# A gated mix of windowed attention and a Mish MLP on one core: tiles read back from DRAM land in the matmul operand itself, and the second half is ordered anew

## The chip, the core and the metric

The kernel runs on one core of a Trainium2 chip. TensorE (PE) multiplies matrices out of SBUF into seven PSUM banks of 128 x 512 fp32; VectorE (DVE), ScalarE (ACT) and GpSimd (POOL) do the elementwise work; SyncE (SP) issues most of the transfers between SBUF and DRAM. Each engine goes through its own list of instructions in order and waits where an instruction needs something that isn't there yet. The metric is the device time of one execution in microseconds.

## The reference

What must be computed, all in fp32, for 2048 tokens of 640 features (x is used by both branches; B_x is not read):

```python
qkv = (x @ wqkv).reshape(B, S, 3, H, Dh)            # 32 heads of 20
idx = pos[:, None] - (jnp.arange(8) * 2)[None, :]   # 8 keys, every second token back
logits = einsum("bhsd,bhswd->bhsw", q, k[idx]) * Dh ** -0.5   # -1e9 where idx < 0
a = einsum("bhsw,bhswd->bhsd", softmax(logits), v[idx]) @ wo
h = x @ w1 + b1                                     # 640 -> 1728
b = (h * tanh(softplus(h))) @ w2                    # Mish, 1728 -> 640
g = sigmoid((x * gate_w).sum(-1, keepdims=True))
out = g * a + (1 - g) * b
```

## The kernel before

**Numbers.** A fp32 product is made of three matmuls in a faster rounding format. Each operand is therefore a *pair*: a tile [128, 2, 512] whose first half (hi) is the rounded value and whose second half (lo) is the rest. `split` makes a pair out of a plain tile: ACT copies it into hi (L400), and DVE or POOL subtracts hi from the plain tile into lo (L403). `mm3` then issues hi by hi (L441), hi by lo (L442) and lo by hi (L443).

**Front half.** The projections of q, k and v, the first MLP layer and the attention run together. The attention is nearly all DVE's (products of 128 x 2560 at L494 and L532, their sums at L497, L542 and L543), 32 pieces of it. The MLP's first layer runs in blocks of 2 x 2 (`quad`) after a Strassen-like scheme with fewer products; ACT copies partial sums from bank to bank between the products (L887) and applies Mish (L695), and for some blocks negates it (L698). Each activation is an activation of another table than the exponential of the softmax (L519), and ACT loads a table (ACT_TABLE_LOAD) where the two meet. The Mish results and sums of them are stored as blocks in DRAM (`act*`, `actt*`). The last 64 of the 1728 columns of a token block are made apart (`mlp1_rest`, "M" and a number in the lists below) in tiles of 64 x 512, whose order of tokens is changed by way of DRAM (`h*`). Sums of w2's quarters (`sums_of_w2`, "S" and a number) go to DRAM too (`s*`).

**Second half.** `mlp2` runs seven products (named a, b, c, e, g, d, f, in this order), each over seven blocks of 128 rows of w2: w2 or its sums (`s*`) as weights, the stored blocks (`act*`, `actt*`) as the moving operand. `load_step` brings in each step's tiles, three steps ahead. A transfer lands in a staging buffer, and `split` makes the pair from it. The last block of three of the products has only 64 rows; there both halves of the tile hold the same 64 rows, one as hi and one as lo, so that two matmuls do for three (`load_low_w`, `load_low_act`, L1207 and L1208). After a product its banks are copied to SBUF (`after_product`, L1106) and, as a start value, back into the bank of a later product. The output projection with wo ("P" and a number, "W") and the gate's rows ("G") come in between, with the stored attention output (`o*`) as moving operand.

**Buffers.** Buffers come from rings: 23 pairs, and as staging 9 `raw`, 3 `hb` and 3 `z`, which also hold Mish results. A buffer is taken again when all that read it is done.

**What sets the order.** `Plan` is a list scheduler with estimated durations. Each engine's tasks are taken by rank, then by when TensorE is estimated to need them; a task of kind "ANY" (mostly lo) goes to DVE or to POOL, whichever the rules `NEAR`, `TURN`, `HOP` give it to. TensorE's tasks come in the order written in the string `FRONT` and, for the second half, in `mlp2`; `BACK` says at which step of `mlp2` the small works are asked for ("1M2": M2 at step 1). Both `EARLY_S` and `HELD` shift when a kind of task may go. All of this is decided when the program is built. On the chip each list is fixed, and semaphores make the waits.

## Time and profile before

| | us |
|---|---|
| median of 3 runs | 624.73 (624.44 to 624.84) |
| the profiled execution | 628.4 |
| its span | 626.3 |
| PE busy, matmul | 617.0 (99%) |
| DVE busy | 565.2 (90%) |
| ACT busy | 384.2 (61%) |
| POOL busy | 255.3 (41%) |

A row of the trace's timeline has the start in us from the span's start, the duration, the engine, the line of the kernel, the operation, output <- inputs, the shape, a count, and in brackets how long the engine was idle before it and what ended that. A row of waits has the waiting operation, the one waited for, the sum in us, how often, and the longest. The durations of matmuls are modelled and overlap; the distance of their starts tells how fast they go. "SPq" is SP's issue of a transfer, and the last number in a row of transfers is the time to its landing. The profiled execution is longer than the median of the others.

### The profile page before, as it was taken

Reading aid. Unit: us, or ns where it says so; the run is one execution under the profiler, and the core shown is the slowest. Engines: PE = TensorE matmul, PEld = TensorE weight load, DVE = VectorE, ACT = ScalarE, POOL = GpSimd, SP = SyncE. Lnnn points to the kernel's source line nnn. Section 1 sums busy time; section 2 is a strip of 40 time slices with the busy share of each in tenths; the row PEclk is TensorE's granted clock in tenths of the full one; section 3 lists DMA queues with packets and bytes.
Section 4 is the critical chain, followed back from the end, with each engine's and each line's share of the span. In section 5 each row is a group of like instructions: output and inputs, shape, how many; then the busy total and the mean of one; then the engine's idle time right before and its main releaser. Section 6 shows DMA issues by size and latency. Waiting matters only on the chain.

```text
span 626.3 us, 8954 instructions
## 1 busy us (share of the span) xinstructions
PE 617.0 (99%) x2717; PEld 509.8 (81%) x2717; DVE 565.2 (90%) x581; ACT 384.2 (61%) x851; POOL 255.3 (41%) x250
## 2 busy tenths in 40 slices
...
GB/s 307 254 200 197 93 235 279 262 255 225 333 265 290 148 289 308 231 203 256 282 295 214 313 211 229 201 239 281 341 332 297 199 259 233 260 252 172 138 1 169
DMA packets 100609, 149.47 MB, mean 239 GB/s; under 512 B 11456, under 2 KB 47296, under 8 KB 100528
## 3 DMA queue, kind: packets, MB, share of 16 engines
...
q8 instruction: 21, 0.34, 0.2%
...
## 4 chain that ended last, share of the span: by engine, by line
PE 87%; DVE 5%; DMA 4%; issue 2%; POOL 1%; ACT 1%; SPq 1%; DVEq 0%; POOLq 0%; ACTq 0%
PE bank L443 28%; PE bank L441 28%; PE bank L442 28%; DMA act<-z 1%; PE bank L587 1%; POOL pair L403 1%; DVE pr L494 1%; DVE pair L403 1%; DMA raw<-act 1%; PE bank L383 1%; PE bank L1208 1%; DMA hb<-act 1%; PE bank L1207 1%; DMA z<-act 0%; DVE pr L542 0%
## 5 line engine op out<-in xcount | busy, mean ns | idle before, releaser
L442 PE MATMUL bank<-pair 128*128 128x512 f32 (+2 forms) x812 | 314.8, 388 | 2.1 <-DVE pair L403 2.0
L441 PE MATMUL bank<-pair 128*128 128x512 f32 (+2 forms) x812 | 314.4, 387 | 0.0
L443 PE MATMUL bank<-pair 128*128 128x512 f32 (+2 forms) x812 | 314.3, 387 | 0.0
L403 POOL TENSOR_TENSOR pair<-raw,pair 128x512 fp32r<-128x512 f32 (+3 forms) x104 | 130.9, 1270 | 190.9 <-DVE side L536 47.3
L442 PEld LDWEIGHTS bank<-pair 128*128 128x128 f32 x812 | 152.5, 188 | 32.8 <-DVE pair L403 3.0
L441 PEld LDWEIGHTS bank<-pair 128*128 128x128 f32 x812 | 152.5, 188 | 30.6 <-ACT bank L887 0.5
L443 PEld LDWEIGHTS bank<-pair 128*128 128x128 f32 x812 | 152.6, 188 | 30.0 <-POOL pair L403 0.2
L400 ACT ACTIVATE pair<-raw 128x512 fp32r<-128x512 f32 (+3 forms) x198 | 117.0, 611 | 44.4 <-DMA raw<-act 19.7
L532 DVE TENSOR_TENSOR pr<-kvq,side 128x2560 f32<-128x2560 f32 x32 | 90.2, 2820 | 1.0
L497 DVE TENSOR_REDUCE lg<-pr 128x128 f32<-128x2560 f32 x32 | 90.1, 2817 | 0.7
L494 DVE TENSOR_TENSOR pr<-kvq,side 128x2560 f32<-128x2560 f32 x32 | 90.1, 2815 | 0.5
L403 DVE TENSOR_TENSOR pair<-raw,pair 128x512 fp32r<-128x512 f32 (+3 forms) x94 | 62.7, 690 | 7.3 <-ACT pair L400 7.0
L593 ACT ACTIVATE kvq<-bank 128x320 f32<-128x320 f32 x64 | 27.9, 437 | 46.8 <-PE bank L443 46.8
L542 DVE TENSOR_TENSOR pr<-pr 128x1280 f32<-128x1280 f32 x32 | 48.7, 1522 | 0.8
L400 ACT ACTIVATE pair<-hb 128x512 fp32r<-128x512 f32 (+2 forms) x40 | 24.7, 617 | 19.8 <-DMA hb<-actt 11.7
L403 POOL TENSOR_TENSOR pair<-hb,pair 128x512 fp32r<-128x512 f32 x12 | 15.6, 1301 | 42.3 <-PE bank L443 12.5
L887 ACT ACTIVATE bank<-bank 128x512 f32<-128x512 f32 x36 | 21.0, 584 | 16.0 <-PE bank L443 15.9
L441 PE MATMUL bank<-kvq,pair 128*128 128x512 f32 x72 | 28.3, 393 | 1.6 <-ACT bank L887 1.6
L443 PE MATMUL bank<-kvq,pair 128*128 128x512 f32 x72 | 28.3, 393 | 0.1
L442 PE MATMUL bank<-kvq,pair 128*128 128x512 f32 x72 | 28.1, 390 | 0.0
L740 POOL TENSOR_TENSOR raw<-raw 128x256 f32<-128x256 f32 (+1 forms) x24 | 20.4, 875 | 17.8 <-DVE side L536 8.2
L683 POOL DMA_DIRECT2D actt<-actt x26 | 22.4, 862 | 12.7 <-DVE pair L403 7.8
...
## 6 DMA issues: line engine op xcount, KB each, us to landing
raw<-in_w SPq DMA_DIRECT2D x34, 256.0 KB, 4.8
raw<-actt SPq DMA_DIRECT2D x30, 256.0 KB, 4.0
...
raw<-in_x SPq DMA_DIRECT2D x29, 256.0 KB, 5.4
actt<-hb SPq DMA_DIRECT2D x28, 256.0 KB, 4.0
act<-z SPq DMA_DIRECT2D x24, 256.0 KB, 6.4
actt<-z SPq DMA_DIRECT2D x24, 256.0 KB, 6.0
raw<-act SPq DMA_DIRECT2D x23, 256.0 KB, 4.7
```

Of the source, the lines that this page charges most:

```text
L400: a = add("ACT", act_ns(n), lambda: A.activation(hi(), raw(), AF.Copy), after, rank=rank, take=take, hold=hold, kind="hi")
L403: return (V if e == "DVE" else G).tensor_tensor(lo(), raw(), hi().bitcast(F32), op=OP.subtract)
L441: nc.tensor.matmul(ps, ah, bh, start=first, stop=False, skip_group_check=more)
L442: nc.tensor.matmul(ps, ah, bl, start=False, stop=False, skip_group_check=more)
L443: nc.tensor.matmul(ps, al, bh, start=False, stop=last, skip_group_check=more)
L494: return V.tensor_tensor(pr, window(kv, s0, 0), qs[:, :, None, :].to_broadcast([128, 2, W, QF]), op=OP.mult)
L497: return V.tensor_reduce(lg_w[:, s0:s0 + 2], pr.rearrange("p s w (h d) -> p s w h d", d=DH), op=OP.add, axis=AX.X)
L532: return V.tensor_tensor(pr.rearrange("p s w (h d) -> p s w h d", d=DH), vw, pw[:, :, :, :, None].to_broadcast([128, 2, W, HQ, DH]), op=OP ...
L542: step("DVE", 1495, lambda: V.tensor_tensor(pr[:, :, 0:4], pr[:, :, 0:4], pr[:, :, 4:8], op=OP.add))
L593: a = add("ACT", 330, lambda: A.activation(kv[:, 7 + s], ps.t[:, QF:3 * QF].rearrange("p (a b) -> p a b", a=2), AF.Copy), [done] + before, ...
L683: return add("POOL", 1200, lambda: G.dma_start(out=blk[key][:rows], in_=src(), accum_op=OP.add, max_dma_last_dim=2048), after, rank=-0.5, ...
L887: return add("ACT", 590, lambda: A.activation(to.t, of.t, AF.Copy), after, rank=-0.6, take=[to], hold=[of], kind=kind)
```

## The change

A class `Landing` gives a loaded tile its place. With `inner` off it is as before: a staging buffer, and a pair that is taken when the split begins. With `inner` on the transfer takes the pair itself and lands in the second half of it; hi is copied out of there, and lo is made over the landed values in place. It is on for what the program itself stored: the Mish blocks, the sums of w2 and the attention output. The program's inputs still land in staging. In `load_low_w` the memset of the unused quarter waits for DVE's subtraction where the tile landed there.

Beside this there are 2 `hb` and 4 `z`, the strings `FRONT` and `BACK` and the numbers `EARLY_S`, `TURN`, `HOP` and `HELD` are new, and the constant 3 of the steps loaded ahead has a name (`DEEP`). Lines after the class have numbers that are 19 higher (L403 is L404, L441 to L443 are L460 to L462, L695 is L714, L887 is L906, L1106 is L1118).

```diff
-SIZES = {"pair": 23, "home": 6, "raw": 9, "hb": 3, "z": 3}
-FRONT = """q1 Q00 s0 w0 Q01 r00 r10 q2 Q10 F0 F1 Q11 r20 r40 T00 T10 Q20 T20 r30 Q21 q3 T30 T40 S0 Q30 w1
-r50 q4 T50 y3 x2 s1 Q31 F2 r01 Q40 F3 M0 T01 r11 r21 q5 r31 r51 M1 T11 S3 Q41 r41 T21 Q50 T31
-Q51 q6 S2 T41 q7 Q60 S1 S4 T51 H Q61 Q70 Q71"""
-BACK = "1M2 1M3 43P4 0S6 2S5 31P1 26W 22G 35P0"
-EARLY_S = 4000
+SIZES = {"pair": 23, "home": 6, "raw": 9, "hb": 2, "z": 4}
+FRONT = """q1 Q00 s0 w0 Q01 r00 q2 r10 r20 Q10 F0 F1 Q11 T00 T10 Q20 r40 S0 T20 r30 Q21 q3 T30 T40 Q30 w1
+r50 y3 q4 T50 x2 s1 Q31 F2 r01 Q40 F3 M0 T01 r11 r21 q5 r31 r51 M1 T11 S3 Q41 r41 T21 Q50 T31
+Q51 q6 T41 S2 q7 Q60 S1 T51 H Q61 Q70 Q71 S4"""
+BACK = "20G 26P1 1S5 6M3 35P0 46P4 18W 1S6 0M2"
+EARLY_S = 2000
+DEEP = 3
...
-    NEAR, TURN, PATIENCE, HOP, STAY, HELD = 4500, 2200, 11000, 3712, 3000, 24502
+    NEAR, TURN, PATIENCE, HOP, STAY, HELD = 4500, 1760, 11000, 3711, 3000, 11176
...
-    def load_pair(src, eng, n=512, rank=SOON, drank=0.0, after=(), wide=False, home=None, cols=1):
-        raw, p = stage(wide), home or pair_buf()
-        d = dma(lambda: raw.t[:, :n].rearrange("p (a f) -> p a f", a=cols) if cols > 1 else raw.t[:, :n], src, after, rank=drank, take=[raw], size=n * 512)
-        p.ready = split(lambda: raw.t[:, :n], lambda: p.t[:, 0, :n], lambda: p.t[:, 1, :n], n, [d], eng, [raw], [p], rank)
-        return p
+    class Landing:
+        def __init__(self, inner, n, home=None, wide=True):
+            self.p, self.n, self.inner = home or pair_buf(), n, inner
+            self.raw = None if inner else stage(wide)
+            self.take = [self.p if inner else self.raw]
+            self.later = [] if inner else [self.p]
+            self.hold = [self.p] if inner else [self.raw, self.p]
+
+        def at(self, rows=slice(0, 128), a=0, b=None):
+            b = self.n if b is None else b
+            return self.p.t[rows, 1, a:b].bitcast(F32) if self.inner else self.raw.t[rows, a:b]
+
+        def split(self, after, eng, rank=SOON):
+            p, n = self.p, self.n
+            return split(self.at, lambda: p.t[:, 0, :n], lambda: p.t[:, 1, :n], n, after, eng, self.hold, self.later, rank)
+
+    def load_pair(src, eng, n=512, rank=SOON, drank=0.0, after=(), wide=False, home=None, cols=1, inner=False):
+        to = Landing(inner, n, home, wide)
+        d = dma(lambda: to.at().rearrange("p (a f) -> p a f", a=cols) if cols > 1 else to.at(), src, after, rank=drank, take=to.take, size=n * 512)
+        to.p.ready = to.split([d], eng, rank)
+        return to.p
...
+        z = add("POOL", 320, lambda: G.memset(p.t[FR:, 1, :n].bitcast(F32), 0.0), [b if inner else a], rank=-0.3, hold=[p])
...
-            p = load_pair(lambda: s_d[kc][:, c:c + 384], "ANY", n=384, wide=i > 2, after=done["s", kc])
+            p = load_pair(lambda: s_d[kc][:, c:c + 384], "ANY", n=384, after=done["s", kc], inner=True)
...
-        acts = [load_pair(lambda P=P: blk[of, P, kc], "ANY", wide=i > 2, after=done[of, P, kc]) for P in range(2)]
+        acts = [load_pair(lambda P=P: blk[of, P, kc], "ANY", after=done[of, P, kc], inner=True) for P in range(2)]
...
-            return load_pair(lambda: o_d[tb][kc * 128:(kc + 1) * 128], "ANY", after=after, drank=0.9, wide=True)
+            return load_pair(lambda: o_d[tb][kc * 128:(kc + 1) * 128], "ANY", after=after, drank=0.9, inner=True)
```

TensorE's list is the same in both, matmul by matmul. What moves is on the other engines. Three places of it follow; a number behind a name counts the buffers made, and the names in brackets are the semaphores that the instruction waits for.

ACT in the front half, about 140 to 148 us into the span: `hb_1547` and `hb_1556` are the same Mish block, and the copy from bank to bank that TensorE waits for there is the one into bank 6. Before:

```order
L400 ACTIVATE pair_1545<-raw_1483 128x128 [waits DMAHW4_49,PE_49]
L695 ACT_TABLE_LOAD
L695 ACTIVATE hb_1547<-bank2_65,bias_77 128x512 [waits DMAHW7_49]
L698 ACTIVATE hb_1547<-hb_1547 128x512 [waits Activation_49]
L887 ACTIVATE bank6_69<-bank3_66 128x512 [waits PE_49]
L500 ACTIVATE side_224<-kvq0_220 128x320 [waits DVE_49]
L695 ACTIVATE z_1528<-z_1528,bias_77 128x512 [waits DMAHW1_49,DMAHW0_49]
L887 ACTIVATE z_1572<-bank0_63 128x512 [waits DMAHW2_49,DMAHW3_49,DMASW2_49,PE_49]
L698 ACTIVATE z_1528<-z_1528 128x512 [waits Activation_49]
L887 ACTIVATE bank4_67<-bank6_69 128x512 [waits PE_49]
```

And now:

```order
L401 ACTIVATE pair_1552<-raw_1451 128x512 [waits DMAHW1_49,PE_49,Pool_49]
L401 ACTIVATE pair_1554<-raw_1485 128x128 [waits DMAHW6_49,PE_49]
L714 ACT_TABLE_LOAD [waits DMAHW5_49]
L714 ACTIVATE hb_1556<-bank2_65,bias_77 128x512 [waits DMASW0_49]
L906 ACTIVATE bank6_69<-bank5_68 128x512 [waits PE_49,Activation_49]
L519 ACTIVATE side_224<-kvq0_220 128x320 [waits DVE_49]
L717 ACTIVATE hb_1556<-hb_1556 128x512 [waits Activation_49]
L906 ACTIVATE z_1581<-bank4_67 128x512 [waits PE_49]
L714 ACTIVATE z_1538<-z_1538,bias_77 128x512 [waits DMASW5_49]
L906 ACTIVATE bank3_66<-bank6_69 128x512 [waits PE_49]
```

The negation of the Mish block (L698, now L717) stood ahead of the copy and now stands behind it.

ACT at the end of product a of the second half, about 409 to 417 us: the rows of L1106, now L1118, take product a's banks to SBUF, and the Mish on `pair_3833` and `pair_3840` before, on `pair_3837` now, is that of the 64 last columns (M2, M3). Before:

```order
L977 ACTIVATE pair_3963<-raw_3918 128x384 [waits DMAHW7_49]
L695 ACT_TABLE_LOAD
L695 ACTIVATE pair_3833<-pair_3833,bias_77 64x512 [waits DMAHW5_49]
L698 ACTIVATE pair_3833<-pair_3833 64x512 [waits Activation_49]
L695 ACTIVATE pair_3840<-pair_3840,bias_77 64x512 [waits DMAHW0_49]
L400 ACTIVATE pair_3995<-raw_3954 128x512 [waits DMAHW2_49,PE_49]
L400 ACTIVATE pair_3999<-z_3757 128x512 [waits DMAHW3_49]
L977 ACTIVATE pair_4023<-raw_3979 128x384 [waits DMAHW6_49,PE_49]
L400 ACTIVATE pair_4026<-hb_3899 128x512 [waits DMAHW4_49,PE_49]
L1106 ACTIVATE kvq1_221<-bank1_64 128x512 [waits DVE_49,PE_49]
L1106 ACTIVATE kvq1_221<-bank2_65 128x512 [waits PE_49]
```

And now:

```order
L528 ACTIVATE lg_223<-bound_78 1x8
L997 ACTIVATE pair_4040<-raw_3897 128x384 [waits PE_49,Activation_49]
L1020 ACTIVATE pair_4053<-hb_3929 128x384 [waits DMAHW0_49,DMAHW1_49,PE_49,Activation_49]
L401 ACTIVATE pair_3997<-pair_3997 128x512 [waits DMAHW4_49]
L1023 ACTIVATE pair_4053<-hb_3929 64x384
L401 ACTIVATE pair_4002<-pair_4002 128x512 [waits DMAHW5_49,Pool_49]
L714 ACT_TABLE_LOAD
L714 ACTIVATE pair_3837<-pair_3837,bias_77 64x512 [waits DMAHW3_49]
L717 ACTIVATE pair_3837<-pair_3837 64x512 [waits Activation_49]
L1118 ACTIVATE kvq1_221<-bank6_69 128x512 [waits DVE_49]
L1118 ACTIVATE kvq1_221<-bank2_65 128x512
L1118 ACTIVATE kvq1_221<-bank0_63 128x512
```

One of the two Mish blocks is gone from here, the other has moved from ahead of four splits to directly ahead of the copies, and other splits stand ahead of it.

SP in the same stretch: the issues about 402 to 405 us before, among which `raw_3896`, `raw_3915`, `hb_3899` and `hb_3932` are staging for the stored blocks of products a and b:

```order
L409 DMA raw_3896<-act11_1_6_98 128x512 [waits DMAHW2_49,Pool_49]
L409 DMA s5_188<-raw_3823 128x128 [waits DMAHW3_49,Activation_49]
L409 DMA hb_3899<-act21_0_2_101 128x512 [waits DMAHW4_49,Pool_49]
L409 DMA pair_3833<-h2_196 64x512 [waits DMAHW5_49,PE_49]
L409 DMA raw_3915<-act21_0_0_99 128x512 [waits DMAHW6_49,DVE_49]
L409 DMA raw_3918<-in_w2 128x384 [waits DMAHW7_49,Pool_49]
L409 DMA pair_3840<-h3_197 64x512 [waits DMAHW1_49,DMAHW0_49,DMASW2_49]
L409 DMA hb_3932<-act21_0_3_102 128x512 [waits Pool_49]
L409 DMA raw_3954<-act21_0_1_100 128x512 [waits DMAHW2_49,Pool_49]
```

And where the same blocks (`act21_0_0`, `act21_0_1`, `act21_0_2`) stand now:

```order
L410 DMA pair_3841<-act11_0_5_90 128x512 [waits DMAHW0_49,PE_49]
L410 DMA pair_3847<-act11_1_5_97 128x512 [waits DMAHW1_49]
L410 DMA pair_3860<-act11_0_6_91 128x512 [waits DMAHW2_49,PE_49]
L410 DMA pair_3862<-act11_1_6_98 128x512 [waits DMAHW3_49,PE_49]
L410 DMA pair_3866<-act21_0_0_99 128x512 [waits DMAHW4_49,PE_49]
L410 DMA pair_3869<-act21_1_0_106 128x512 [waits DMAHW5_49,PE_49]
L410 DMA pair_3873<-act21_0_1_100 128x512 [waits DMAHW6_49,PE_49]
L410 DMA pair_3885<-act21_1_1_107 128x512 [waits DMAHW7_49,PE_49]
L410 DMA pair_3890<-act21_0_2_101 128x512 [waits DMAHW0_49,PE_49]
```

They go into pairs, wait for TensorE (the last matmul that read the slot) and not for DVE or POOL, and stand ahead of the transfers of `h2` and `h3` (the M blocks) that they stood behind.

72 lines of the change are left out of this document (33 added, 39 removed).

## The prediction

> **What bounds the kernel now.** I read the page first, then PE's waits, then windows of 20 us, then the matmuls around each window that is short.
>
> ```profile
> PE 617.0 (99%) x2717; PEld 509.8 (81%) x2717; DVE 565.2 (90%) x581; ACT 384.2 (61%) x851; POOL 255.3 (41%) x250
> ```
>
> TensorE is busy for 617.0 of a span of 626.3 us. The change keeps each of its matmuls, in the same order and shapes, so its work stays and only its gaps can go or come. The waits of PE, and three of the windows (columns: us, then busy PE, PEld, DVE, ACT, POOL, each with its instructions, the granted clock, the DMA share, GB/s), say where they are:
>
> ```profile
> PE bank L442 <- DVE pair L403: 2.0, 1, 2.0
> PE bank L441 <- ACT bank L887: 1.6, 1, 1.6
> ...
> 140.00:160.00 20.00, 18.41 (x82) 15.01 (x81) 17.00 (x17) 14.61 (x29) 11.57 (x16) 1.00 0.88 248
> 400.00:420.00 20.00, 18.02 (x79) 14.55 (x78) 16.70 (x18) 12.01 (x23) 8.19 (x9) 1.00 0.74 206
> ```
>
> Two waits, one about 145 us on an ACT copy of a bank and one about 412 us on a DVE subtraction, make most of what can be had. Small ones don't show as idle, because a modelled matmul is 0.39 us long and the next begins 0.227 us after it; they show in the distance of starts (the row at 411.41 follows one at 411.19 by 0.22). The five places that the change can touch:
>
> ```profile
> 144.64 0.39 PE L443 MATMUL bank<-kvq,pair 128*128 128x512 f32 x1
> 146.61 0.50 PE L441 MATMUL bank<-kvq,pair 128*128 128x512 f32 x1 [1.59 <-ACT bank L887]
> 146.95 0.40 PE L442 MATMUL bank<-kvq,pair 128*128 128x512 f32 x1
> ...
> 178.76 0.39 PE L443 MATMUL bank<-pair 128*128 128x512 f32 x1
> 179.17 0.50 PE L441 MATMUL bank<-pair 128*128 128x512 f32 x1
> ...
> 411.19 0.39 PE L443 MATMUL bank<-pair 128*128 128x512 f32 x1
> 411.41 0.39 PE L441 MATMUL bank<-pair 128*128 128x512 f32 x1
> 413.78 0.50 PE L442 MATMUL bank<-pair 128*128 128x512 f32 x1 [1.98 <-DVE pair L403]
> ...
> 423.89 0.39 PE L441 MATMUL bank<-pair 128*128 128x512 f32 x1
> 424.43 0.50 PE L442 MATMUL bank<-pair 128*128 128x512 f32 x1
> ...
> 500.27 0.39 PE L443 MATMUL bank<-pair 128*128 128x512 f32 x1
> 500.67 0.47 PE L1207 MATMUL bank<-pair 128*128 128x512 f32 x1
> 501.39 0.47 PE L1208 MATMUL bank<-pair 128*128 128x512 f32 x1 [0.25 <-DVE pair L1013]
> ```
>
> Distance less 0.227: 1.74 at 144.64, 0.18 at 178.76, 2.14 at 411.41, 0.31 at 423.89, 0.17 and 0.49 about 500. The matmul after such a wait also comes 0.11 late (146.61 to 146.95 is 0.34), so the stalls are 1.85, 0.29, 2.25, 0.42 and, about 500 without that, 0.66: 5.5 us.
>
> **The change part by part.** *Landing in place.* A loaded tile of the second half now waits for a pair slot instead of for a staging buffer, and its low half is made over itself. The operations are the same:
>
> ```profile
> L403 POOL TENSOR_TENSOR pair<-raw,pair 128x512 fp32r<-128x512 f32 (+3 forms) x104 | 130.9, 1270 | 190.9 <-DVE side L536 47.3
> L403 DVE TENSOR_TENSOR pair<-raw,pair 128x512 fp32r<-128x512 f32 (+3 forms) x94 | 62.7, 690 | 7.3 <-ACT pair L400 7.0
> ...
> 408.11 0.63 ACT L400 ACTIVATE pair<-raw 128x512 fp32r<-128x512 f32 x1 [2.16 <-DMA raw<-act]
> ...
> raw<-act SPq DMA_DIRECT2D x23, 256.0 KB, 4.7
> ```
>
> What changes is when a load can go. The stall at 411.41 has its cause here: ACT's row at 408.11 waited 2.16 us for a load that left late, and DVE's subtraction came behind it. In the new order the loads of that product stand ahead of it by the whole product before (the third of the places shown with the change), the slots of all loads used between 390 and 435 were freed 19 us or more before that use (the freeing matmuls of the new order at the times that they had in this trace), and their subtractions have moved to POOL. So 2.25 at 411.41 and 0.42 at 423.89 go. At 500 the low rows are split in another place of DVE's queue: I count all 0.66 as gone. Bounds of the three together: 3.33 gone, or (the subtraction at 500 is no earlier) 2.67. Whether a subtraction in place takes longer no row shows; I take 0.69 and 1.27 us on, bounded by nothing and by 10% of one at the end of a chain, 0.13.
>
> *ACT's new order at 414, the wait that takes the place.* After product a, two banks are copied to SBUF and back before product b may add to them. Before, the table load and Mish of one token block came ahead of all that, in the time that ACT had while waiting. Now these stand behind two splits whose pair slots the matmuls about 410.5 free, and directly ahead of the copies:
>
> ```profile
> 410.50 0.39 PE L443 MATMUL bank<-pair 128*128 128x512 f32 x1
> ...
> 409.16 0.51 ACT L977 ACTIVATE pair<-raw 128x384 fp32r<-128x384 f32 x1
> 409.69 1.28 ACT L695 ACT_TABLE_LOAD   x1
> ```
>
> The second of these slots is free at 410.50 + 0.39 = 410.9. From there ACT has four copies at 0.53 each (409.16 to 409.69, start to start) = 2.1, the table load with what follows it 1.30, Mish 0.72 and its negation 0.53 (rows at 143.43, 144.73 and 145.45 in the next fence), and the first bank copy 0.58 (row at 145.98): 410.9 + 5.2 = 416.1. The matmul that needs it is the twelfth after 411.41, so without the old stall it could start at 411.41 + 12 × 0.227 = 414.13. A stall of 1.9 us, where 2.25 goes away. Bounds: 0.8 if the four copies are not all ahead of it in fact and overlap more; 2.5 if the copy also waits for DVE, whose attention product must have left the buffer it writes.
>
> By the Trainium skill (ScalarE: Activation LUTs, What ACT_TABLE_LOAD costs) a switch of tables is about 1.28 us of load and 1.38 us of drain, 2.66 in all. The trace agrees on the load (1.28) and shows no drain behind it: Mish begins 0.02 us later (143.43 + 1.28 to 144.73). By the page the stall would be an estimated 3.3 us instead of 1.9, and the two table loads that ACT has more in the whole kernel would cost 5.3 us of an engine with 39% to spare instead of 2.6.
>
> *ACT's order in the first half.*
>
> ```profile
> 143.10 0.31 ACT L400 ACTIVATE pair<-raw 128x128 fp32r<-128x128 f32 x1 [2.34 <-DMA raw<-in_w]
> 143.43 1.28 ACT L695 ACT_TABLE_LOAD   x1
> 144.73 0.69 ACT L695 ACTIVATE hb<-bank,bias 128x512 f32<-128x512 f32 x1
> 145.45 0.63 ACT L698 ACTIVATE hb<-hb 128x512 f32<-128x512 f32 x1
> 145.98 0.58 ACT L887 ACTIVATE bank<-bank 128x512 f32<-128x512 f32 x1
> ...
> 83.78 0.58 ACT L887 ACTIVATE bank<-bank 128x512 f32<-128x512 f32 x1
> ...
> 85.14 0.39 PE L441 MATMUL bank<-kvq,pair 128*128 128x512 f32 x1
> ...
> 130.41 1.28 DVE L403 TENSOR_TENSOR pair<-raw,pair 128x512 fp32r<-128x512 f32 x2
> ...
> 131.72 0.39 PE L443 MATMUL bank<-kvq,pair 128*128 128x512 f32 x1
> ```
>
> At 145.98 the copy stood behind a load that landed late, a table load, Mish and the negation. The negation (145.45 to 145.98, 0.53 us) now comes behind the copy, and the small load ahead of it all goes up to 0.9 us earlier: between 0.5 and 1.4 of the 1.85, I take 0.8, since the load's landing is unsure. At 178 the table load and Mish move behind the copy: 0.29 gone. At 85 the copy now follows a table load and would end at about 85.25 where PE wants it at 85.14: +0.15 (0 to 0.3). At 131 the subtractions come up to 0.9 later, behind one more addition and an output of the attention, and the first had 0.6 to spare: +0.25 (0 to 0.5). About 404, while the splits of product a go between POOL and DVE anew, I see subtractions with 0.3 to 1.5 us to spare: +0.3 (0 to 1.5).
>
> Sum in the profiled execution: −3.33 + 1.9 − 0.8 − 0.29 + 0.15 + 0.25 + 0.3 = −1.82. It took 628.4 us (626.3 and 2.1 around it), 3.67 over the median of 624.73. If that excess is spread evenly, all of the 1.82 is left in the median: 622.9. If it lies in the waits (5.5 us of them, and 0.6 more that the change doesn't touch; 6.1 − 3.67 = 2.4 would be left) the gain is 0.4 of it, 0.7: 624.0. I take the middle, 1.3 less: **623.4 us**, and 622.3 to 624.7 as this case's own range.
>
> **The rivals.** *The old waits go and none comes.* For it: ACT is busy for only 12.01 of the 20 us from 400, so its copies may come early enough. Against it: four splits and a table load that can't begin before 410.9. Then the sum is −3.7, in the median between 1.5 and 3.7 less: 622.1.
>
> *The waits are the profile's own.* Plain executions, 3.67 us shorter, may hardly have them. Then removing and adding them both count little: 624.0 to 624.8, say 624.5. Speaking against it: a chain of a load, a split and a subtraction has fixed lengths without the profiler too.
>
> *Slower: pair slots gate the loads.* Before, 15 staging buffers beside 23 pairs took loads ahead. Now a load of the second half goes when PE has freed one of the 23.
>
> ```profile
> 471.03 0.39 PE L443 MATMUL bank<-pair 128*128 128x512 f32 x1
> ...
> 480.10 0.39 PE L441 MATMUL bank<-pair 128*128 128x512 f32 x1
> ...
> 395.98 5.60 SPq L409 DMA_DIRECT2D h<-pair  x8
> ```
>
> The tightest load that I found is freed by the matmul at 471.03 and read by that at 480.10: 9.1 us. It needs the landing (4.7), the split (0.53) and a subtraction on POOL (1.27), 6.5. The 2.6 left last unless something holds SP's queue: eight issues in a row took it 5.60 us at 395.98. From 2.6 us of delay on, each late load stalls PE, and about eleven loads between 468 and 557 have less than 12 us: the one 5.6 us block on the tightest costs 3.0: 626.4 with the forecast's other terms. Against it: the median such load has 15 us.
>
> *Slower by DVE and POOL holding each other up.* This is by a rule: the subtractions that move to POOL run beside DVE's 2.82 us products.
>
> ```profile
> 395.95 2.82 DVE L494 TENSOR_TENSOR pr<-kvq,side 128x2560 f32<-128x2560 f32 x1
> ...
> 396.15 1.02 POOL L403 TENSOR_TENSOR pair<-raw,pair 128x384 fp32r<-128x384 f32 x1 [4.17 <-DVE kvq L545]
> 397.14 1.29 POOL L403 TENSOR_TENSOR pair<-hb,pair 128x512 fp32r<-128x512 f32 x1
> ```
>
> Two subtractions ran on POOL inside one such product, in 1.02 and 1.29 us, as anywhere else. Were POOL kept out until the product ends, each one that meets it would be up to 2.8 late, and with two or three us to spare about 413 one such delay on the path is about 2 us: 625.5. The Trainium skill (SBUF — State Buffer, SBUF: two separate sides) says that an operation of DVE with two inputs in SBUF and one of GpSimd that reads SBUF share a port pair as an exclusive lock, the later one waiting for the whole instruction. The two rows speak against that here.
>
> **How the numbers follow.** The forecast 0.44, no new wait 0.19, waits of the profile alone 0.18, slots 0.15, lock 0.04. A measurement of this kernel can tell 0.2%, 1.25 us, from no change: below 623.48 counts as faster, above 625.98 as slower. Of the forecast a little over half is faster, the rest the same; of the second nearly all is faster, of the third nearly all the same; of the fourth most is slower. With a tenth of the forecast's uncertainty on the slow side: faster 0.45, same 0.37, slower 0.18. The range for 8 in 10 runs from the second case's middle less some (621.3, half of its gain beyond 622.1 being left out) to just short of the slot case's price (626.2).
>
> **What would show it.** Right: PE's waits on a DVE subtraction near 412 and at the low rows about 501 are gone; a wait of 1 to 2.5 us on ACT's bank copy (L1118) stands at about 414; that on the seed copy near 145 is under 1.4. PE's busy time remains 617 within 1 and the stretch after 430 has no gaps. Wrong: any wait of PE on a DMA or a split landing in a pair after 435 (slots); POOL subtractions longer than 1.3 us beside DVE's products (lock); no wait at 414 (the second case); the same stalls in the profile's differences but no difference in the median (the third).

## The result, and the profile after

The changed kernel takes 632.63 us (median of 6 runs, 630.98 to 636.08) against 624.79 for the kernel before (6 runs, 624.21 to 629.58): a ratio of 1.0118, 95% interval 1.0079 to 1.0156. It is slower, by 7.4 us from this ratio and by 7.8 between the medians, where the forecast had 623.4 and a range up to 626.2. The profiled execution took 632.53 us (span 630.8); that of before took 628.4.

TensorE's work is the same, its waits are not. The page's first part and the waits of PE in the changed kernel:

```profile
PE 618.5 (98%) x2717; PEld 510.6 (81%) x2717; DVE 560.0 (89%) x575; ACT 390.3 (62%) x853; POOL 263.5 (42%) x256
```

```profile
PE bank L460 <- ACT kvq L1118: 5.2, 1, 5.2
...
PE bank L460 <- ACT bank L906: 0.6, 2, 0.4
PE bank L460 <- ACT bank L1286: 0.4, 1, 0.4
```

The two old waits (2.0 on a lo part, 1.6 on the bank copy at 145) are gone or small. One wait of 5.2 us stands in their place, on L1118, the copy of product a's banks to SBUF, at the place and on the engine that the forecast named. The windows show that this is not all of it:

```profile
400.00:420.00 20.00, 14.80 (x62) 11.83 (x61) 18.66 (x18) 11.39 (x21) 10.54 (x9) 0.93 0.82 238
420.00:440.00 20.00, 20.00 (x82) 16.30 (x81) 16.71 (x18) 13.01 (x23) 9.15 (x8) 0.90 0.83 253
```

From 420 PE is busy for all of 20 us and yet does 82 matmuls where it did 88 before: the granted clock is 0.93 and 0.90 in these two windows, where it was 1.00. The second of these windows in the kernel before:

```profile
420.00:440.00 20.00, 19.85 (x88) 16.09 (x88) 19.20 (x28) 12.41 (x24) 4.41 (x8) 1.00 0.95 281
```

The matmuls themselves show where the slow clock begins and ends:

```profile
412.10 0.39 PE L462 MATMUL bank<-pair 128*128 128x512 f32 x1
417.69 0.79 PE L460 MATMUL bank<-pair 128*128 128x512 f32 x1 [5.20 <-ACT kvq L1118]
418.28 0.63 PE L461 MATMUL bank<-pair 128*128 128x512 f32 x1
418.71 0.63 PE L462 MATMUL bank<-pair 128*128 128x512 f32 x1
...
423.40 0.60 PE L461 MATMUL bank<-pair 128*128 128x512 f32 x1
423.83 0.41 PE L462 MATMUL bank<-pair 128*128 128x512 f32 x1
```

The distance from 412.10 to 417.69 is 5.59, 5.36 over the usual 0.227. Behind it the matmuls stand 0.43 apart (418.28 to 418.71) until 423.83, and this loses another 2.96 us. The place costs 8.3 us; the forecast had 1.9.

PE's list is the same in both kernels, so each matmul's start can be subtracted from its partner's in the profiled execution of before. The difference moves in steps (negative: earlier than before):

| place (us in before) | forecast | profiled execution |
|---|---|---|
| 5, clock's warm-up at the start | nothing | −1.22 |
| 76 | nothing | +0.66 |
| 85 | +0.15 | +0.38 |
| 131 | +0.25 | 0 |
| 145 | −0.8 | −1.41 |
| 178 | −0.29 | −0.30 |
| 404 | +0.3 | 0 |
| 411 | −2.25 | −2.25 |
| 414, the new stall | +1.9 | +5.36, and +2.96 of slow clock |
| 424 | −0.42 | −0.42 |
| 500 | −0.66 | −0.75 |
| 551 to 554 | nothing | +0.73 |

The first row is of this execution alone: between the second profiles of the two kernels, further below, it is 0.

ACT's own rows say why the new stall is so long:

```profile
409.18 0.53 ACT L1020 ACTIVATE pair<-hb 128x384 fp32r<-128x384 f32 x1 [0.82 <-DMA h<-pair]
412.90 0.63 ACT L401 ACTIVATE pair<-pair 128x512 fp32r<-128x512 f32 x1 [3.19 <-DMA pair<-act]
413.43 0.51 ACT L1023 ACTIVATE pair<-hb 64x384 fp32r<-64x384 f32 x1
413.85 0.61 ACT L401 ACTIVATE pair<-pair 128x512 fp32r<-128x512 f32 x1
414.48 1.28 ACT L714 ACT_TABLE_LOAD   x1
415.77 0.72 ACT L714 ACTIVATE pair<-pair,bias 64x512 f32<-64x512 f32 x1
416.52 0.63 ACT L717 ACTIVATE pair<-pair 64x512 f32<-64x512 f32 x1
417.06 2.02 ACT L1118 ACTIVATE kvq<-bank 128x512 f32<-128x512 f32 x4
```

These are the instructions that the forecast added up, in its order and at its durations: from 412.90 to PE's start at 417.69 they take 4.79. What it didn't have is the 3.19 us before them, in which ACT stands still until a stored block (`pair<-act`) has landed. The chain of waits and SP's rows follow that transfer back (SPq rows are the issues):

```profile
409.03 3.84 DMA pair<-act
412.90 0.63 ACT pair L401
```

```profile
405.44 0.45 SPq L410 DMA_DIRECT2D h<-pair  x1
408.08 0.34 SPq L410 DMA_DIRECT2D raw<-in_wo  x1
408.47 0.46 SPq L410 DMA_DIRECT2D pair<-h  x1
409.03 1.00 SPq L410 DMA_DIRECT2D pair<-act  x2
...
SPq L410 <- DMA s<-raw: 2.1, 1, 2.1
```

The block was issued at 409.03 and landed 3.84 us later, near the usual (3.4 in the median of such transfers). It was issued late, because SP stood before the load of a tile of wo (408.08) for 2.1 us: that load takes a staging buffer from which a sum of w2 (`s<-raw`) was still being written to DRAM. An estimate of what this is worth: 2.1 us earlier, and with the same 3.84, the block would have landed about 410.8, 1.1 us after ACT was done with the split at 409.18. So the hold makes two thirds of the 3.19, and the block's place in the list the rest.

The landing in place leaves staging free, the planner gives it to loads of wo, and in SP's list three of these now stand ahead of the two blocks; one holds the queue. That it is the landing which moves them, the two halves of the change show, which are run alone further below: wo's loads go out from 469 to 479 us before, from 367 to 418 with the landing alone, from 410 to 462 with the new settings alone, and from 353 to 412 with both.

### The profile page after: what moved, and what is told of

It reads as the page before. It is cut to its first block, busy times and chain, and to the rows that moved or that the text cites. A ratio compares the mean times of both kernels' runs of the same rounds, so it can differ in the third digit from the quotient of the medians.

```text
span 630.8 us, 8954 instructions
## 1 busy us (share of the span) xinstructions
PE 618.5 (98%) x2717; PEld 510.6 (81%) x2717; DVE 560.0 (89%) x575; ACT 390.3 (62%) x853; POOL 263.5 (42%) x256
## 4 chain that ended last, share of the span: by engine, by line
PE 82%; DVE 10%; ACT 4%; DMA 2%; issue 2%; DVEq 0%; SPq 0%; ACTq 0%
PE bank L460 27%; PE bank L462 27%; PE bank L461 27%; DVE pr L513 3%; DVE lg L516 2%; ACT pair L401 1%; DVE pr L551 1%; DMA pair<-actt 1%; PE bank L606 1%; DVE raw L759 1%; DVE pr L561 1%; DVE pair L404 1%; DMA pair<-act 1%; ACT L714 1%; PE bank L1220 0%
## 5 line engine op out<-in xcount | busy, mean ns | idle before, releaser
L460 PE MATMUL bank<-pair 128*128 128x512 f32 (+2 forms) x812 | 315.8, 389 | 6.0 <-ACT kvq L1118 5.2
L462 PE MATMUL bank<-pair 128*128 128x512 f32 (+2 forms) x812 | 315.4, 388 | 0.0
L460 PEld LDWEIGHTS bank<-pair 128*128 128x128 f32 x812 | 153.2, 189 | 37.4 <-ACT kvq L1118 5.6
L462 PEld LDWEIGHTS bank<-pair 128*128 128x128 f32 x812 | 153.2, 189 | 30.5 <-POOL pair L404 0.2
L404 POOL TENSOR_TENSOR pair<-raw,pair 128x512 fp32r<-128x512 f32 (+4 forms) x77 | 96.9, 1271 | 112.2 <-issue 24.3
L401 ACT ACTIVATE pair<-pair 128x512 fp32r<-128x512 f32 (+2 forms) x139 | 81.5, 614 | 58.6 <-DMA pair<-act 30.4
L404 POOL TENSOR_TENSOR pair<-pair 128x512 fp32r<-128x512 f32 (+1 forms) x52 | 64.3, 1254 | 103.6 <-DVE pair L404 34.5
L401 ACT ACTIVATE pair<-raw 128x512 fp32r<-128x512 f32 (+3 forms) x119 | 69.4, 610 | 11.0 <-PE bank L462 3.7
L404 DVE TENSOR_TENSOR pair<-pair 128x512 fp32r<-128x512 f32 (+2 forms) x87 | 55.0, 672 | 9.8 <-ACT pair L401 9.4
L759 POOL TENSOR_TENSOR raw<-raw 128x256 f32<-128x256 f32 (+1 forms) x27 | 24.0, 896 | 28.2 <-DMA raw<-in_x 10.5
L404 DVE TENSOR_TENSOR pair<-raw,pair 128x512 fp32r<-128x512 f32 (+3 forms) x42 | 30.4, 751 | 5.8 <-ACT pair L401 5.8
L906 ACT ACTIVATE bank<-bank 128x512 f32<-128x512 f32 x36 | 21.0, 583 | 14.4 <-PE bank L462 14.0
L460 PE MATMUL bank<-kvq,pair 128*128 128x512 f32 x72 | 28.5, 395 | 0.3 <-ACT bank L906 0.2
L462 PE MATMUL bank<-kvq,pair 128*128 128x512 f32 x72 | 28.3, 393 | 0.1
```

Of the source, the lines that this page charges most:

```text
L401: a = add("ACT", act_ns(n), lambda: A.activation(hi(), raw(), AF.Copy), after, rank=rank, take=take, hold=hold, kind="hi")
L404: return (V if e == "DVE" else G).tensor_tensor(lo(), raw(), hi().bitcast(F32), op=OP.subtract)
L460: nc.tensor.matmul(ps, ah, bh, start=first, stop=False, skip_group_check=more)
L462: nc.tensor.matmul(ps, al, bh, start=False, stop=last, skip_group_check=more)
L759: return (V if e == "DVE" else G).tensor_tensor(t.t[:, i:i + n], a.t[:, j:j + n], b.t[:, k:k + n], op=op)
L906: return add("ACT", 590, lambda: A.activation(to.t, of.t, AF.Copy), after, rank=-0.6, take=[to], hold=[of], kind=kind)
```

## The experiments

The theory after this comparison: the new stall is ACT's list (bank copies behind splits that wait for late blocks, behind a table load and Mish), made longer by SP's queue, and the clock adds to it. The rivals: the loss comes from the pair slots, or from the new settings altogether, or from the clock alone.

Two sorts of kernels follow. Some change a rule and let the planner deal all lists anew. Others keep every list of every engine as it was dealt for the changed kernel and move only the rows named; in those, line numbers are 154 higher (L401 is L555, L460 to L462 are L614 to L616, L1118 is L1272), 153 in the one with GpSimd's waits taken away. All are compared with the kernel before, which was timed anew beside each group (medians 625.07 to 625.91).

### Planner variants: copies first, M2 behind them, wo loads later

```diff
+        if i == 11:
+            for a in acts:
+                for c in copies:
+                    behind(a.ready[0], c)
...
+                        copies.append(z.done)
                         seed(("u", P, j), z, [z.done])
+                        behind(m2[0], z.done)
```

The first lines make the two splits wait for the copies, the last one M2's Mish.

> The changed kernel, but M2's Mish and the two splits of product b's fifth block are made to come behind the four copies of product a's banks in ACT's list. Nothing is left out. Theory 1 (the 5.4 us gap of TensorE at 412 is ACT's list: two splits that wait for late loads, a table load and Mish ahead of the first bank copy; and the slow matmuls behind it follow from the gap): the copy starts when the two splits behind PE's slots are done, about 410.2, so no gap at 412 and no matmul at 0.43 us distance; the time falls by 8.3 us against the changed kernel, to about 624.3, and is equal to before within 0.3%. Theory 2 (landing in place costs elsewhere, by slots or POOL, and the gap is only where it shows): the gap moves to another place within the next 50 us, and the time stays above 629. Theory 3 (the gap is the copy's wait for DVE's attention product, which must have left the buffer that it writes): gap unchanged.

Measured: 635.31 (632.47 to 636.16), ratio 1.0146 (1.0119 to 1.0172). The gap at 412 is gone. Others came: at 403 and at 465, each with a slow stretch behind it, and at 441. By the words of the expectation that is theory 2. But this kernel has other lists than the changed one from there on, so it can't tell what the landing costs from what the new deal costs; the runs with kept lists below can.

The second variant has only the line on M2:

> The changed kernel with M2's table load, Mish and negation alone behind the four bank copies; the splits that wait for late loads stay ahead. Nothing is left out. Theory 1: of the gap of 5.4 us the 2.6 us of table load, Mish and negation go and 2.5 to 3.0 us stay (the split at 412.9 still waits for its load, the copy ends at about 415.0). If the slow matmuls depend on how long TensorE idles, a gap of 2.7 us may leave the clock full, as 2.1 us did before: then 627 us or less; with a slow stretch 629. Theory 2: 630 or more. Theory 3: gap unchanged, 632.

Measured: 636.35 (633.64 to 637.31), ratio 1.0163 (1.0131 to 1.0195). The stall at 412 shrinks to 3.33 us and has no slow clock behind it; gaps at 440 and at 462 are new, the latter with a slow stretch behind it.

```diff
-        wide = [load_pair(lambda kc=kc: wo[kc][:, :512], "ANY", wide=True) for kc in range(KC)]
+        wide = [load_pair(lambda kc=kc: wo[kc][:, :512], "ANY", drank=2.0, wide=True) for kc in range(KC)]
```

> The changed kernel with wo's loads of a lower rank in SP's list, so that three of the four that stood ahead of product b's fifth block stand behind it. ACT's list keeps the two splits, table load, Mish and negation ahead of the bank copies. Nothing is left out. Theory 1, with the late loads as half of its cause: the loads land about 409.5 instead of 412.9, ACT's chain from 409.2 is then two splits' halves (1.0), table load 1.3, Mish 0.7, negation 0.5, copy 0.6, so the copy ends at 413.3 and the gap is 1.0 to 1.5 us, at full clock: 625 to 626 us. If wo's loads are not what delays them (the round trip of M2 through DRAM is), the gap stays above 4 us and the time above 631.

Measured: 632.64 (630.62 to 633.06), ratio 1.0102 (1.0068 to 1.0136). The gap is 3.07 with 1.6 of slow clock; 1.40 came at 404, 0.61 at 260 and 1.5 about 550.

What follows: whatever lets ACT copy earlier, or the blocks land earlier, shortens the gap at 412. But when the planner deals anew, other places become short, so the time of these three says nothing on what the one gap costs. Their traces say more on the clock. In the first, a wait of 1.88 is followed by 3.4 us of slow matmuls:

```profile
405.49 0.50 PE L461 MATMUL bank<-pair 128*128 128x512 f32 x1 [1.88 <-DVE pair L404]
...
406.35 0.63 PE L461 MATMUL bank<-pair 128*128 128x512 f32 x1
...
409.34 0.53 PE L462 MATMUL bank<-pair 128*128 128x512 f32 x1
409.71 0.39 PE L460 MATMUL bank<-pair 128*128 128x512 f32 x1
```

In the second, a wait of 3.17 is not (starts 0.34 and then 0.23 apart):

```profile
415.92 0.50 PE L460 MATMUL bank<-pair 128*128 128x512 f32 x1 [3.17 <-ACT kvq L1124]
416.26 0.39 PE L461 MATMUL bank<-pair 128*128 128x512 f32 x1
416.49 0.40 PE L462 MATMUL bank<-pair 128*128 128x512 f32 x1
```

### Gaps of a known length

In the kernel before, chains of 4 to 10 small copies on ACT were put in front of seven steps of the second half, to make gaps of about 2.4 to 5.5 us. This kernel does work that the reference doesn't need.

```diff
+DELAY = {("e", 2): 5, ("e", 4): 8, ("g", 2): 6, ("g", 4): 9, ("d", 2): 7, ("d", 4): 10, ("f", 2): 4}
...
+                        last = add("ACT", 530 * DELAY[name, c], waste, [last, z_scratch], rank=-2.0)
```

> The kernel before, with TensorE made to wait at seven places of the second half for a chain of 4 to 10 dummy copies on ACT (4 in product f, 5 and 8 in e, 6 and 9 in g, 7 and 10 in d; each copy 0.52 us, start to start), so gaps of about 2.4, 2.9, 3.4, 3.9, 4.4, 5.0 and 5.5 us. Nothing is left out. If the length of the gap sets the clock, gaps up to some length between 2.1 and 5.2 us are followed by matmuls 0.23 us apart, and longer ones by a stretch of about 6 us at 0.43 us (2.6 to 3 us lost each). If the slow stretch at 418 had another cause (the stretch of work, its neighbours), no gap here shows it. Time: 624.8 + 27 of gaps + 3 per slow stretch, 652 to 666 us.

Measured: 647.34 in one execution. The copies read nothing of TensorE's, so PE did not wait for them; they held ACT up instead, and two gaps of 7.4 and 8.2 us came out, each with a slow stretch of 3.4 us behind it. It tells that gaps of this length end in a slow clock, and nothing on where it begins.

### The four bank copies alone

Every list as dealt for the changed kernel; in ACT's, the four copies of product a's banks go ahead of the two splits, the table load and Mish:

```diff
+L1272 ACTIVATE kvq_221<-bank_69 128x512
+L1272 ACTIVATE kvq_221<-bank_65 128x512
+L1272 ACTIVATE kvq_221<-bank_63 128x512
+L1272 ACTIVATE kvq_221<-bank_64 128x512
 L555 ACTIVATE pair<-pair 128x512
 L1177 ACTIVATE pair<-hb 64x384
 L555 ACTIVATE pair<-pair 128x512
 L868 ACT_TABLE_LOAD
 L868 ACTIVATE pair<-pair,bias 64x512
 L871 ACTIVATE pair<-pair 64x512
-L1272 ACTIVATE kvq_221<-bank_69 128x512
-L1272 ACTIVATE kvq_221<-bank_65 128x512
-L1272 ACTIVATE kvq_221<-bank_63 128x512
-L1272 ACTIVATE kvq_221<-bank_64 128x512
```

> The changed kernel with every list of every engine as it is, but for one place of ACT's: the four copies of product a's banks stand ahead of product b's two late splits, the table load, Mish and negation, right behind the split of the 64-row weights. (In the runs before this one the scheduler dealt all later lists anew, so that gaps could come from there.) Nothing is left out. Theory 1 (ACT's list makes the gap at 412): the copies end between 410.3 and 412, the 5.4 us gap and the 3 us of slow clock behind it go, no new gap within 30 us, and the time falls by 8 us to 624.3 (not more than 0.3% from before). Theory 2 (landing in place costs elsewhere): the time stays above 629, with gaps of TensorE on splits of landed tiles behind 412.

Measured: 629.07 (626.4 to 632.37, 12 runs), ratio 1.0046 (1.0024 to 1.0069). Four rows of one engine take away 0.7% of the 1.2%. Neither theory holds whole: the gap at 412 and its slow clock are gone, as theory 1 had it, but the median is a hair over the 629 of theory 2, and 0.87 us at 436 (on a lo part) and 0.30 at 443 are new. The profiled execution has a gap that those of the changed kernel lack: 2.4 us in two pieces at 403, with 1.7 of slow clock.

```profile
405.87 0.61 PE L615 MATMUL bank<-pair 128*128 128x512 f32 x1 [1.88 <-DVE pair L558]
```

No list differs ahead of this place, so what varies is when the loads land (ACT stood 1.36 us for one at 400.69). Of the 12 runs five, from 628.73 up, have a granted clock of 0.996 like the profiled one, and the four fastest, 626.4 to 627.83, have 0.998 or more. Whether it is this gap that divides them isn't shown, since plain runs leave no trace here.

### The loads on time alone

The same lists, and in SP's the two loads of stored blocks go ahead of three loads of wo, two stores and M2's way by DRAM:

```diff
 L564 DMA s_188<-raw 128x256
+L564 DMA pair<-act_0_4_103 128x512
+L564 DMA pair<-act_1_4_110 128x512
 L564 DMA hb<-in_wo 128x512
...
 L564 DMA pair<-h_196 64x512
-L564 DMA pair<-act_0_4_103 128x512
-L564 DMA pair<-act_1_4_110 128x512
 L564 DMA h_197<-pair 32x2x128 x3
```

> The changed kernel with every list as it is, but for one place of SP's: the two loads of product b's fifth block stand ahead of three loads of wo, two stores and M2's way through DRAM instead of behind them. ACT's list keeps the two splits, table load, Mish and negation ahead of the bank copies. Nothing is left out. If the loads' place in SP's queue is what made the predicted gap of 1.9 us one of 5.4: the loads land at about 409 instead of 412.9, ACT's chain runs from 409.7 without a wait, the copy ends at about 414.4 and the gap is 1.7 to 2.2 us, with no or one short slow stretch behind it; the time is 626 to 628. If the chain waits for something else (M2's way through DRAM, which now starts later), the gap stays over 4 us and the time over 631.

Measured: 628.79 (627.88 to 629.73), ratio 1.006 (1.0038 to 1.0082).

```profile
416.74 0.63 PE L614 MATMUL bank<-pair 128*128 128x512 f32 x1 [2.54 <-ACT kvq L1272]
```

With the blocks on time the gap is 2.71 (a wait of 2.54) instead of 5.36. ACT's rows show the chain that was forecast:

```profile
410.88 0.53 ACT L1174 ACTIVATE pair<-hb 128x384 fp32r<-128x384 f32 x1 [0.82 <-PE bank L616]
411.31 0.62 ACT L555 ACTIVATE pair<-pair 128x512 fp32r<-128x512 f32 x1
...
414.82 0.72 ACT L868 ACTIVATE pair<-pair,bias 64x512 f32<-64x512 f32 x1 [0.66 <-DMA pair<-h]
```

The first split begins when its pair slot comes free, the three others follow it without a wait, and from 410.88 to PE's start at 416.74 it takes 5.86. Of this, 0.66 is Mish waiting for M2's tile, whose way through DRAM the edit put later; the other 5.20 are the 5.2 of the forecast. Without that wait the gap would be about 2.05, near the forecast's 1.9, and near 5.36 − 3.19 = 2.17. The chain of splits, table load, Mish and copy is thus worth what was worked out, and the rest of the stall is the late landing, by SP's queue. The slow clock behind it costs 1.7 instead of 2.96, and a gap of 1.35 stands at 402. This run and the one before it take each cause away alone; both gain.

### Each half of the change alone

Landing in place with the settings of before, and the new settings with all tiles in staging:

```diff
-SIZES = {"pair": 23, "home": 6, "raw": 9, "hb": 2, "z": 4}
+SIZES = {"pair": 23, "home": 6, "raw": 9, "hb": 3, "z": 3}
...
-BACK = "20G 26P1 1S5 6M3 35P0 46P4 18W 1S6 0M2"
-EARLY_S = 2000
+BACK = "1M2 1M3 43P4 0S6 2S5 31P1 26W 22G 35P0"
+EARLY_S = 4000
...
-    NEAR, TURN, PATIENCE, HOP, STAY, HELD = 4500, 1760, 11000, 3711, 3000, 11176
+    NEAR, TURN, PATIENCE, HOP, STAY, HELD = 4500, 2200, 11000, 3712, 3000, 24502
```

> The landing in place alone: buffers, the strings of the order and the planner's numbers as before the change. The scheduler deals the lists with them. Nothing is left out. Theory 1: what counts is what stands ahead of product a's bank copies in ACT's list; here these are three splits of loads of product b, without table load and Mish, so a gap of 0 to 3 us at 412 and a time of 623 to 628. Theory 2: landing in place costs by itself, 629 to 635.

```diff
         def __init__(self, inner, n, home=None, wide=True):
+            inner = False
             self.p, self.n, self.inner = home or pair_buf(), n, inner
```

> The new buffers, strings and planner's numbers alone: every tile lands in staging as before. Nothing is left out. Theory 1: the table load, Mish and one split whose load has long landed stand ahead of the bank copies, so the gap there is 0 to 1.5 us; the gains of the first half stay (1.7 us); the old waits on late staging loads (411, 424) may come back: 623 to 628. Theory 2: about equal to before or better, since the cost comes with the landing.

Measured: 640.04 (ratio 1.0218, 1.0192 to 1.0244) and 646.43 (1.0307, 1.0274 to 1.034). Waits of PE in the first:

```profile
PE bank L460 <- ACT kvq L1118: 5.9, 1, 5.9
PE bank L460 <- ACT bank L1286: 3.4, 1, 3.4
```

and in the second:

```profile
PE bank L461 <- ACT pair L401: 10.6, 3, 6.9
PE bank L462 <- DVE pair L404: 2.7, 1, 2.7
```

Both are far above what was expected (623 to 635 by either theory). The landing by itself brings the stall on the bank copies, 5.9 us, with the old settings too: it doesn't need the new ones. There the last split ahead of the copies waited 4.24 us for its block, with no table load and no Mish behind it. The order without the landing starves PE of hi parts, 1.6 us at 412 and 6.9 and 2.2 between 462 and 478, and the granted clock is 0.53 from 466 to 484. Each half is worse than both together: the settings were dealt for lists with the landing in them, so the two times don't add up, and neither is the price of its half.

### More rows put right

To the four bank copies were added: two lo parts of DVE at 404 ahead of sums of w2, and bank copies at 76, 85 and 557 ahead of what stood before them ("five places"); then lo parts of DVE at 131 and, with attention's output, at 431, and ACT's seed copy at 552 ("eight places"). Two of the rows:

```diff
+L1060 ACTIVATE bank_69<-bank_65 128x512
 L868 ACT_TABLE_LOAD
 L868 ACTIVATE hb<-bank_67,bias 128x512
-L1060 ACTIVATE bank_69<-bank_65 128x512
...
+L558 TENSOR_TENSOR pair<-raw,pair 128x384
+L558 TENSOR_TENSOR pair<-pair 128x512
 L1133 TENSOR_TENSOR raw<-raw 128x256
 L1152 SCALAR_TENSOR_TENSOR pair<-hb,pair 128x384
 L1133 TENSOR_TENSOR raw<-raw 128x256
-L558 TENSOR_TENSOR pair<-raw,pair 128x384
-L558 TENSOR_TENSOR pair<-pair 128x512
```

> As the run with four rows up, and four more places of the changed lists: two subtractions of product a move up in DVE's list past two sums of w2 and a split that waits for ACT (the gap at 404 that two of the runs showed), and three bank copies move up in ACT's list past Mish (the gaps of 0.66, 0.38 and 0.64 us at 76, 85 and 557). Nothing is left out. Theory 1: of the changed kernel's gains (2.3 at 411, 1.4 at 145, 0.3 at 178, 0.4 at 424, 0.75 at 500, against before's profile) all stay and nothing is given back: 1 to 3 us below before, 622 to 624. Theory 2: above 629.

> The lists of the run with five places, and three more: in DVE's a subtraction at 131 moves up past an output of the attention, and a subtraction at 431 and an output of the attention move up past a subtraction that waits for a late load; in ACT's the seed copy at 552 moves up past a split that waits for a late load. Nothing is left out. If the rest of the changed kernel's loss is such places, one row that waits for a load ahead of one that TensorE needs: the gaps of 0.67 us at 131, 2.13 at 431, 0.39 at 440 and 0.91 at 552 go, and the time is 622 to 625, 1 to 3 us below before. If new gaps come as fast as old ones go (the load on DVE and the transfers limit it), 626 to 628.

Measured: 627.39 (ratio 1.0024, 1.0003 to 1.0045) and 626.1 (624.42 to 632.08; 1.0027, 1.0005 to 1.0049). The eight-place kernel's profiled execution took 624.62, under both of before; but the median stays 0.27% over.

> The eight-place kernel profiled a second time. If its median above its first profile (626.1 against a profiled 624.62 us) comes from waits that are there only in some executions, this profile shows tensor-engine gaps over 0.5 us that the first lacked (at 404, 435 to 442, 460 or 552) or a second stretch of the slow clock; if not, its gaps sum again to about 1.3 us after the start and its time is 624 to 625.

> The same kernel a third time, to tell a chance gap from one that returns: a gap that stands in the second and the third profile at the same matmul is a row of the lists that is still short by some tenths of a us; gaps that change their places are DMA landings that vary, and no row moved would take them away.

Measured: 625.79 and 624.29. Gaps of 0.36 to 0.39, of 0.53 to 0.55 and of 0.26 to 0.45 return in all three executions at the same matmuls (79, 440, 553). The one at 435 is there with 0.05, 1.46 and 0.66. PE's waits in the second execution, and then in the third:

```profile
PE bank L1374 <- POOL pair L558: 1.2, 1, 1.2
```

```profile
PE bank L1374 <- POOL pair L558: 0.4, 1, 0.4
```

The expectation had two cases, and both hold in part: rows still short by some tenths, and one place that goes with the landings.

### Before and after, profiled again

> The kernel before, for a second profile. If the gaps of the first profile (1.85 us at 145, 2.25 at 411, 0.42 at 424, 0.77 at 500) belong to the kernel, they are here again, within 0.5 us each. If they are of that execution alone (it took 628.4 us where the median is 624.8), the ones that hang on a transfer, at 145 and 411, are shorter by 1 us or more.

> The changed kernel, for a second profile, and timed beside the others. The gap at 412 is here again, 4 to 6 us with a slow stretch behind it, if it belongs to the kernel. A gap at 404 of 1 to 3 us, as in three of the other runs with the same lists up to there, would say that the first profile lacked it by chance. Time 631 to 634.

Measured: 626.23 for before, and for the changed kernel 634.42 (633.67 to 635.11, ratio 1.015, 1.0128 to 1.0171). Before's waits in its second execution:

```profile
PE bank L442 <- DVE pair L403: 1.5, 1, 1.5
...
PE bank L441 <- ACT bank L887: 0.8, 1, 0.8
```

The stall at 145 is 1.10 where it was 1.85, that at 411 is 1.75 where it was 2.25, that at 500 is gone, and only 0.42 at 424 is the same. So of the five stalls, 5.5 us in the first execution, 3.6 are left in one that is 2.2 us shorter (1.10, 0.29 at 178 as before, 1.75 and 0.42). In the changed kernel the new stall is there again, and longer:

```profile
414.94 0.63 ACT L401 ACTIVATE pair<-pair 128x512 fp32r<-128x512 f32 x1 [4.22 <-DMA pair<-act]
```

ACT stood 4.22 us for the block this time, and PE waited 6.2.

These two executions can be laid over each other, matmul by matmul, like the first two. PE's last matmul comes 6.96 us later: −3.12 at 145, 178, 411 and 424, +1.8 at 76, 85 and 552, and +8.3 at the new stall with its slow clock (6.38 and 1.9). At the start there is no difference.

### The same repair on the kernel before

Before's lists, with the rows moved ahead that its own gaps waited for: bank copies at 145 and 178 ahead of the table load and Mish; at 410 two splits and the bank copies ahead of the table load and Mish; lo parts of DVE for 411 and 424 (line numbers 153 higher than in the kernel before):

```diff
+L1040 ACTIVATE bank_69<-bank_66 128x512
 L848 ACT_TABLE_LOAD
 L848 ACTIVATE hb<-bank_65,bias 128x512
 L851 ACTIVATE hb<-hb 128x512
-L1040 ACTIVATE bank_69<-bank_66 128x512
...
+L556 TENSOR_TENSOR pair<-raw,pair 128x512
+L556 TENSOR_TENSOR pair<-hb,pair 128x512
+L556 TENSOR_TENSOR pair<-z,pair 128x512
 L696 TENSOR_TENSOR pr<-pr 128x2x320
-L556 TENSOR_TENSOR pair<-hb,pair 128x512
-L556 TENSOR_TENSOR pair<-raw,pair 128x512 x2
```

> The lists of the kernel before, every row as it was dealt, with only those rows moved ahead that its own gaps waited for: the bank copies at 145 and 178 ahead of the table load and Mish, the splits and four bank copies at 410 ahead of the table loads and Mishes, the DVE parts for 411 and 423. If the rows are what holds the tensor engine, the time is 621.5 to 623, some 2 to 3.5 us under before. If its gaps of 145, 411 and 500 are mostly of the profiled executions (its second profile had 1.10, 1.75 and 0), the time is within 0.1% of before.

Measured: 629.47 (628.17 to 631.15), ratio 1.0075 (1.0055 to 1.0095). Neither case held: it is slower. The gap at 411 is gone, as it should be, and new ones of 2.2 us at 422 and 1.8 at 430 more than pay it back. The one at 145 goes too, but 1.3 us of it come back at 149, and 0.5 is new at 188. The two behind 411:

```profile
422.26 0.50 PE L594 MATMUL bank<-pair 128*128 128x512 f32 x1 [1.23 <-ACT pair L553]
423.61 0.50 PE L595 MATMUL bank<-pair 128*128 128x512 f32 x1 [0.85 <-DVE pair L556]
...
430.85 0.49 PE L594 MATMUL bank<-pair 128*128 128x512 f32 x1 [1.05 <-ACT pair L553]
```

At both, ACT's split began within 0.1 us of the landing of its block. PE came earlier, the blocks did not: the split for 430 began at 430.17, where it began at 428.69 and 426.62 in the two profiles of before. So the idle time of a gap is no measure of what its removal gains: a later transfer may have lived on it. Why this block landed even later than before is not shown.

### GpSimd's waits, and DVE's rows instead

The rows that still stood in the eight-place kernel's profiles were taken in two ways. The planner makes a lo part on GpSimd wait for the end of a certain instruction of DVE. The first kernel drops this wait for five such parts (one at 79, two at 431, two at 440); no buffer needs it. Both move the lo part at 553 ahead of attention's output. The second keeps the waits and at 431 moves rows of DVE instead:

```diff
-L558 TENSOR_TENSOR pair<-pair 128x512 x2
-L718 TENSOR_TENSOR kvq_220<-pr 128x320
-L558 TENSOR_TENSOR pair<-pair 128x512
+L558 TENSOR_TENSOR pair<-pair 128x512
+L718 TENSOR_TENSOR kvq_220<-pr 128x320
+L558 TENSOR_TENSOR pair<-pair 128x512 x2
```

> The eight-place lists with the waits that still stood in all three of its profiles taken away: five GpSimd lo parts (one at 79, two at 431, two at 440) no longer wait for the end of the vector instruction that the planner put before them, and the vector engine's lo of 553 stands ahead of attention's output. If these rows are what the kernel still loses, its gaps at 79, 431, 440 and 553 are under 0.2 each, its profile is 623 to 624.5 us, and its median 624 to 625, level with before. If plain executions vary by landings that no row moves, the profile gains and the median stays at 625.5 to 626.5. If a lo part that runs beside a vector instruction slows, its rows are over 1.3 us and nothing is gained.

> The eight-place lists with every GpSimd wait for the vector instruction before it kept, and three vector rows moved instead: at 431 the lo of pair_4045 and attention's output go ahead of the lo whose load lands late, at 440 one lo goes ahead of three others, at 553 one lo goes ahead of attention's output. If the waits are what keeps GpSimd's lo parts off the vector instructions that they block, no small vector instruction beside a lo part grows (its rows stay at 0.3 and 0.7 us, where the kernel without the waits had 3.38 and 2.45), the gaps at 431 to 435 and 553 are under 0.5, and the profile is 623 to 625.5 us. The median is then at or a little under that of the eight-place kernel, 625 to 626; it is under before only if the landings leave the rows alone.

Measured: 628.23 (626.58 to 631.83; ratio 1.0039, 1.0016 to 1.0062) and 628.55 (625.75 to 630.45; 1.004, 1.0021 to 1.006). Both are over the eight-place kernel's 626.1, with intervals that overlap its own. Four lo parts of DVE in a row, first in the eight-place kernel's first profile, then with GpSimd's waits dropped:

```profile
432.78 2.49 DVE L558 TENSOR_TENSOR pair<-pair 128x512 fp32r<-128x512 f32 x4
```

```profile
434.07 2.77 POOL L557 TENSOR_TENSOR pair<-pair 128x512 fp32r<-128x512 f32 x2
...
434.95 4.25 DVE L557 TENSOR_TENSOR pair<-pair 128x512 fp32r<-128x512 f32 x4
```

The four take 4.25 us instead of 2.49 when GpSimd's two run beside them; the first of them ended at 437.40, 0.56 after GpSimd was done at 436.84. In the second kernel, with all waits kept, it is 4.69, beside GpSimd's 3.31: two of the four, at 435, took 1.78 each. A sum of 128x128 at 425, 0.28 us elsewhere and in the second kernel too, took 3.38 in the first beside two parts of GpSimd. So the waits keep the two apart at 425 but not at 435, and the rows that still looked free of charge were not. A version faster than before did not come out of this.

## Why the prediction was wrong, and where it was right

**The chain at 414: right place, a landing left out.** The step that failed is "From there ACT has four copies at 0.53 each": it lets the four run on end from 410.9, when the second pair slot comes free. The first of them did begin there. The matmul that frees the slot starts at 408.70 here, 1.80 earlier than before, and ACT's split at 409.18, 0.09 after the slot is free by the forecast's own reckoning (its row names a store that it waits for too; with the loads on time the row of the same instruction names the matmul). But the next one splits a stored block, and stood 3.19 us until that had landed, 4.22 in the second execution. The step took the slot for the last thing that the copies wait for; no term of the sum holds the landing of the two blocks. The instructions behind it, their order and their durations held (4.79 us from the first late split to PE). With the loads on time the chain took the 5.2 us of the forecast and the stall was 2.71, 0.66 of it another tile's landing; the bounds, 0.8 to 2.5, would nearly have held. The part on the landing in place had even said that the loads "stand ahead of it by the whole product before". That was so for the first blocks of the product, shown with the change; it was not looked at for the last two, behind the loads of wo.

**The clock: no term of the sum.** The stall was priced as idle time only. The 2.96 us of slow matmuls behind it are the second largest item of the profiled execution, and 1.6 to 1.7 us came behind smaller gaps of other kernels.

**The small places.** At 178, 411 and 424 the terms held to 0.01; 145 gained 1.41 instead of 0.8, at its bound of 1.4; 500 gained 0.75 for 0.66. At 85 the change cost 0.38, over its bound of 0.3, and at 131 and 404 nothing, for 0.25 and 0.3. Not forecast were 0.66 at 76 and 0.73 at 551 to 554, two more copies behind work of ACT's new order: I had looked at the copies which PE waited for before, not at all those which the new order moves.

**From the profile to plain runs.** The forecast took the middle between an excess spread evenly and one that lies in the waits. The second profile of before supports the latter: shorter by 2.2 us, it has 2.0 less stall at the touched places. So the gains, 5.1 against the first execution (1.41, 0.30, 2.25, 0.42, 0.75), are 3.1 against one nearer the median, while the new stall with its slow clock cost 8.3 in both profiles of the changed kernel (5.36 and 2.96; 6.38 and 1.9). The sum in plain terms is thus −3.1 of old stalls, +1.8 of the small ones at 76, 85 and 551 to 554, and +8.3: +7.0, which is what the second profiles differ by (6.96), and near the 7.8 between the medians. The −1.22 at the start is left out: the second pair doesn't have it.

**The rivals.** *No new wait* fell. *Waits of the profile alone* was right for a part of the old stalls and wrong for the new. *Pair slots gate the loads* fell as it stood: no wait on a load in a pair after 435. Its mechanism, something that holds SP's queue, is what happened, but by way of the staging which the change freed, some 60 us earlier and on other tiles. *DVE and POOL holding each other up* was given 0.04 because two rows showed GpSimd's parts unhindered inside a long product. Here a short operation of the changed kernel's DVE, and GpSimd beside it:

```profile
388.60 2.45 DVE L561 TENSOR_TENSOR pr<-pr 128x1280 f32<-128x1280 f32 x1
...
388.41 1.29 POOL L404 TENSOR_TENSOR pair<-pair 128x512 fp32r<-128x512 f32 x1 [1.36 <-ACT pair L401]
```

The sum that takes 1.49 us in other executions took 2.45, its start lying inside GpSimd's row. Counted over all short operations of DVE (each against the median of its line and shape), such excess is 10.7 us in before and 8.8 in the changed kernel, 11.1 and 8.6 in the second profiles. DVE thus loses less by it than before, and the new stall has another cause; but the reason given against this rival was wrong. The rule of the Trainium skill (SBUF — State Buffer, Who interferes with whom), by which the later of two such operations stands still for the whole of the other, agrees with these rows for DVE's short operations. It does not show for the long products with a broadcast input, beside which GpSimd's parts ran in their usual time, and the two rows I had chosen were of those.

What stays open: why plain executions of the eight-place kernel are 0.27% over before when its three profiled ones (624.3 to 625.8) lie within those of before. The place at 435 varies by 1.4 us with the landings, and one of 12 runs took 632.08 at a clock of 0.994; whether such gaps make the median couldn't be seen, since plain runs leave no trace here.
